# Per-bucket sums with the operands of TensorE exchanged, and a transpose in the last part

## The chip, the cores and the metric

The kernel runs on one core of a Trainium2 chip. The metric is the device time of one execution in microseconds; a kernel's time is the median of several timed runs. A further execution is profiled, and the views of the profile that are shown come from that one execution.

## The reference

The kernel computes one layer of a tensor-product message passing network on a graph with N = 10000 nodes and E = 640000 edges. Each node has a 64 x 4 matrix of features (C = 64 channels, M = 4 components), and all data is fp32.

```python
R = silu(edge_feat @ w_rad)                          # (E, C)
xs = x[src]                                          # (E, C, M)
tp = einsum('eci,ef,ifo->eco', xs, Y, cg)            # (E, C, M)
msg = R[:, :, None] * tp
agg = segment_sum(msg.reshape(-1, C * M), dst, N).reshape(N, C, M)
return einsum('ncm,cd->ndm', agg, w_mix)
```

The kernel doesn't form `tp` edge by edge. For each node n it first sums the outer product of R * x[src] (64 x 4 = 256 numbers) with Y (4 numbers) over the edges that end in n, and applies `cg` and `w_mix` afterwards, once for each node.

## The kernel before

The edges are first sorted by their destination. Two passes do this: `pass1` sorts the edges into groups of 576 nodes (18 buckets), `pass2` sorts each group into its 18 buckets of 32 nodes. Both use `route`: one-hot matrices (made at lines 546, 552 and 553) move the edges' payloads with matmuls on TensorE (line 560), and an indirect DMA from the GpSimd queue stores the moved rows (line 571). An edge's payload is nine words: a key, the four of Y and the four edge features.

The edges are taken in three parts (26%, 47% and 27% of them; `SPLIT`), so that the sorting of one part can run beside the sums of another. In `messages` the work is cut into units. A unit is one bucket's worth of 4 (first and second part) or 5 (last part) tiles of 128 edges; in the second part a bucket has two units. There are 313 buckets, so 313 + 626 + 313 = 1252 units with 5321 tiles in all. For a unit k the stages are:

- `gather`: one indirect DMA a tile from the GpSimd queue fetches x[src] into `xg` (line 785), six units ahead; there are eight buffers of `xg`.
- `turn`, `turned`, `radial`, `silu`: the payload is transposed on TensorE (line 798), copied on ScalarE (803), multiplied with `w_rad` on TensorE (808) and put through SiLU on ScalarE (811).
- `spots`: VectorE makes `S` = onehot(dst) * Y (lines 819 and 822), 32 nodes by 4 = 128 columns a tile.
- `products`: VectorE multiplies `xg` by R in place (line 829); the result is called `V`, 256 columns a tile.
- `sums`: TensorE adds up V^T S over the unit's tiles into `G` in PSUM (line 840). V is the stationary operand, in two halves of 128 columns (32 channels each), and S the moving one, so each tile takes two matmuls. `G` holds channel and component on the partitions and nodes by f on the columns.
- `fetch`, `evict`: `G` leaves PSUM. In the first part ScalarE copies it (line 871); in the second and last part VectorE adds the sum that was kept from the part before (line 869), which `fetch` has read from DRAM (854). After the first and second part the sum goes back to DRAM (873). In the last part it goes into `Gs`, which collects four buckets.
- `full`, `mix`, `mixed`: in the last part, once `Gs` has four buckets, TensorE multiplies it with the combined weights of `cg` and `w_mix` (line 888), ScalarE copies the result (896) and SP stores it.

The order of TensorE, VectorE and ScalarE is written out by hand in this stretch: the program emits the stages in four quarters for each k, each stage for its own unit k + a, and between two quarters `groups` inserts steps of the sorting. Within an engine the instructions run in that order. The quarters are, before the change:

```python
        quarters = (((index, LI), (gather, LG), (fetch, 4), (turn, 2), (sums, 0), (silu, 1)), ((turned, 2), (spots, 1)),
                    ((products, 1), (evict, 0)), ((radial, 2), (full, -1)))
```

`G` has one PSUM buffer, so the sum of the next bucket waits until the last one is evicted. Waits between engines are set by the framework, from the tiles that instructions read and write.

Of the kernel before, what the change touches and what calls it, by code (L numbers as in the profile page):

```python
# [18 lines left out]
F = mybir.dt.float32  # L19
# [3 lines left out]
AF = mybir.ActivationFunctionType  # L23
AX = mybir.AxisListType

P = 128
B = 18
# [4 lines left out]
NB = 32  # L32
# [3 lines left out]
SPLIT = ((0.26, (4,)), (0.47, (4, 4)), (0.27, (5,)))  # L36
LG = 6
LI = 8
# [33 lines left out]
class Kernel:  # L72
    def __init__(self, ctx, tc, x, src, dst, Y, ef, w_rad, cg, w_mix, out):
# [53 lines left out]
        self.p1.dst = self.dr.tile([self.p1.rows, self.p1.rw], F, name="grp")  # L127
        self.p2.dst = self.dr.tile([self.p2.rows, self.p2.rw], F, name="bkt")

        self.sums = self.dr.tile([self.NBK, P, 256], F, name="sums")  # L130
        self.in_group = {"grp": 0, "bkt": 0}
        self.tab = {}
        self.held, self.wanted, self.pos = None, False, None
# [607 lines left out]
    def messages(self):  # L741

        nc, ph = self.nc, self.ph
        units = [((k, g), j, s) for k, g in self.segs for j in range(self.nb(g)) for s in range(len(SPLIT[k][1]))]
        MT = max(sum(u) for _, u in SPLIT)
        n = len(units)
        IDX, XG, PRE, ST_, RT, SS, VS, GP, GS, OLD = ({} for _ in range(10))

        def quad(k):

# [4 lines left out]
        def tiles(k):  # L755

            g, j, s = units[k]
            u = SPLIT[g[0]][1]
            return sum(u[:s]), u[s]
# [71 lines left out]
        def sums(k):  # L831
            g, j, s = units[k]
            ut = tiles(k)[1]
            if s == 0:
                GP[g, j] = self.ps.tile([P, 2, NB, 4], F, name="G", tag="G", bufs=1)
            G = GP[g, j]
            V, S = VS.pop(k), SS.pop(k)
            for t in range(ut):
                for h in range(2):
                    nc.tensor.matmul(G[:, h].rearrange("p n f -> p (n f)"),  # L840
                                     V[:, t, 32 * h:32 * h + 32, :].rearrange("p c i -> p (c i)"),
                                     S[:, t].rearrange("p n f -> p (n f)"),
                                     start=(s + t + h == 0), stop=(last(k) and t == ut - 1),
                                     skip_group_check=True)

        def last(k):
            return units[k][2] == len(SPLIT[units[k][0][0]][1]) - 1

        def fetch(k):

            g, j, s = units[k]
            if g[0] and s == 0:
                OLD[g, j] = ph.tile([P, 2, 4, NB], F, name="old", bufs=4)
                nc.sync.dma_start(OLD[g, j].rearrange("p h f n -> p (h f n)"), self.sums[g[1] * B + j])

        def evict(k):
            g, j, s = units[k]
            if not last(k):
                return
            final = g[0] == len(SPLIT) - 1  # L860
            if not final:
                to = ph.tile([P, 2, 4, NB], F, name="Gp")
            else:
                if j % 4 == 0:
                    GS[g, j // 4] = ph.tile([P, 2, 4, 4, NB], F, name="Gs")
                to = GS[g, j // 4][:, :, :, j % 4, :]
            G = GP.pop((g, j)).rearrange("p h n f -> p h f n")
            if g[0]:
                nc.vector.tensor_tensor(to, OLD.pop((g, j)), G, op=OP.add)  # L869
            else:  # L870
                nc.scalar.activation(to, G, AF.Copy)
            if not final:
                nc.sync.dma_start(self.sums[g[1] * B + j], to.rearrange("p h f n -> p (h f n)"))

        def full(k):
            g, j, s = units[k]
# [15 lines left out]
        def mixed(k, po):  # L892
# [4 lines left out]
            nc.sync.dma_start(self.out[n0:n0 + nn, :], ot[:nn])  # L897


        quarters = (((index, LI), (gather, LG), (fetch, 4), (turn, 2), (sums, 0), (silu, 1)), ((turned, 2), (spots, 1)),  # L900
                    ((products, 1), (evict, 0)), ((radial, 2), (full, -1)))
        todo, po = [], None
        for k in range(-LI, n + 3):
            for stages in quarters:
# [218 lines left out]
```

## Time and profile before

| what | value |
|---|---|
| timed runs, median of 3 | 10905.27 us (10901.35 to 10920.43) |
| profiled execution, its own time | 10989.96 us |
| its span | 10987.9 us |
| granted TensorE clock, mean | 0.834 of full speed |
| busy: PE, PEld, DVE, ACT, POOL | 8420.1, 7126.3, 7056.8, 4102.8, 6003.7 us |
| matmul passes and weight loads | 52157 each |
| indirect gathers of x | 5321 |

PE is TensorE's matmuls and PEld its weight loads, which overlap them; DVE is VectorE, ACT is ScalarE, POOL is GpSimd, SP is the queue of the direct DMAs. Matmuls are pipelined, so that the busy time of PE is more than the time its columns take. In the groups of instructions a row gives line, engine, operation, what is written from what, shapes, how often, then busy time and the mean of one in ns, then the idle time of the engine just before and what ended it. "issue" is idle time in which the engine waited for nothing that the profile shows, "remote" a wait whose end is not put down to an instruction. An fp32 matmul shows as two passes, each with a weight load.

### The profile page before, as it was taken

Reading aid. Unit: us, or ns where it says so; the run is one execution under the profiler, and the core shown is the slowest. Engines: PE = TensorE matmul, PEld = TensorE weight load, DVE = VectorE, ACT = ScalarE, POOL = GpSimd, SP = SyncE. Lnnn points to the kernel's source line nnn. Section 1 sums busy time; section 2 is a strip of 40 time slices with the busy share of each in tenths; the row PEclk is TensorE's granted clock in tenths of the full one; section 3 lists DMA queues with packets and bytes.
Section 4 is the critical chain, followed back from the end, with each engine's and each line's share of the span. In section 5 each row is a group of like instructions: output and inputs, shape, how many; then the busy total and the mean of one; then the engine's idle time right before and its main releaser. Section 6 shows DMA issues by size and latency. Waiting matters only on the chain. (4 is left out here: it accounts for less than half of the span.)

```text
span 10987.9 us, 150963 instructions
## 1 busy us (share of the span) xinstructions
PE 8420.1 (77%) x52157; PEld 7126.3 (65%) x52157; DVE 7056.8 (64%) x13530; ACT 4102.8 (37%) x12301; POOL 6003.7 (55%) x6286
## 2 busy tenths in 40 slices
PE   6767787777877777777767777777767888888886
PEld 5656676666765666666656666666656666666665
DVE  7767777777766666666656666665546655656553
ACT  5645454554543433333333333333313222222220
POOL 1235455555555555555555556565566666666664
PEclk8878888888888888888888788888878888888887
DMA  7222222222223333333333333333333333333332
GB/s 155 77 62 80 83 84 86 83 82 85 87 84 93 96 99 98 99 98 99 99 94 97 92 95 102 98 103 97 96 110 103 106 107 107 104 104 107 107 103 86
DMA packets 695214, 1057.15 MB, mean 96 GB/s; under 512 B 251068, under 2 KB 499025, under 8 KB 694448
## 3 DMA queue, kind: packets, MB, share of 16 engines
q0 software_dynamic: 285872, 746.46, 23.6%
q1 hardware_dynamic: 405984, 294.29, 9.6%
q8 instruction: 413, 6.77, 0.3%
q10 hardware_dynamic: 2592, 6.74, 0.2%
q14 instruction: 353, 2.89, 0.1%
HBM read 856.14 MB, written 206.13 MB: 97 GB/s over the span
## 5 line engine op out<-in xcount | busy, mean ns | idle before, releaser
L785 POOL DMA_INDIRECT xg<-in_x_dram,sidx x5321 | 5052.2, 949 | 3344.1 <-issue 1371.8
L840 PE MATMUL G<-S,xg 128*128 128x128 f32 x21284 | 3250.8, 313 | 681.0 <-issue 395.4
L840 PEld LDWEIGHTS G<-S,xg 128*128 128x128 f32 x21284 | 3053.5, 226 | 797.3 <-issue 461.7
L560 PE MATMUL pr<-X,oh 128*128 128x126 f32 (+1 forms) x21252 | 3097.7, 306 | 604.6 <-ACT rt L567 294.1
L560 PEld LDWEIGHTS pr<-X,oh 128*128 128x128 f32 x21252 | 2929.4, 217 | 800.6 <-issue 384.2
L829 DVE TENSOR_TENSOR xg<-xg,pre 128x1024 f32<-128x1024 f32 (+1 forms) x1252 | 1603.8, 1281 | 866.8 <-ACT pre L811 705.8
L537 DVE TENSOR_TENSOR X<-dv,Wt 128x1485 f32<-128x1485 f32 (+3 forms) x941 | 1596.0, 1696 | 699.4 <-remote 413.2
L552 ACT ACTIVATE sq<-i,rowf 128x128 f32<-128x128 f32 x5640 | 1743.6, 393 | 5.6 <-DVE rowf L524 4.8
L811 ACT ACTIVATE pre<-pre 128x256 f32<-128x256 f32 (+1 forms) x1252 | 477.5, 381 | 2998.4 <-remote 990.0
L808 PE MATMUL pre<-wr,sT 36*128 36x256 f32 (+1 forms) x2504 | 1020.4, 490 | 310.1 <-ACT sT L803 256.4
L822 DVE TENSOR_TENSOR S<-dv,pay 128x512 f32<-128x512 f32 (+1 forms) x1252 | 907.6, 725 | 280.0 <-remote 131.0
L553 ACT ACTIVATE oh<-sq,ones 128x768 f32<-128x768 f32 (+1 forms) x941 | 928.5, 987 | 152.9 <-remote 50.9
L571 POOL DMA_INDIRECT grp<-rt,idx x417 | 415.2, 996 | 921.3 <-ACT rt L567 498.7
L571 POOL DMA_INDIRECT bkt<-rt,idx x524 | 524.8, 1002 | 646.6 <-ACT rt L567 422.0
L546 DVE TENSOR_TENSOR oh<-dv,rowf 128x768 f32<-128x768 f32 (+2 forms) x939 | 803.5, 856 | 0.3 <-PE pre L798 0.2
L808 PEld LDWEIGHTS pre<-wr,sT 36*128 36x128 f32 (+1 forms) x2504 | 414.6, 206 | 514.4 <-ACT sT L803 290.3
L567 ACT ACTIVATE rt<-pr 128x135 f32<-128x135 f32 (+1 forms) x941 | 253.6, 270 | 1075.9 <-remote 636.0
L869 DVE TENSOR_TENSOR Gs<-old,G 128x256 f32<-128x256 f32 x313 | 131.5, 420 | 766.5 <-PE G L840 277.9
L798 PE MATMUL pre<-ident,pay 128*36 128x128 f32 (+1 forms) x1252 | 383.2, 306 | 129.1 <-DVE xg L829 97.5
L798 PEld LDWEIGHTS pre<-ident,pay 128*36 128x36 f32 (+1 forms) x1252 | 132.7, 106 | 515.0 <-issue 235.5
L507 ACT ACTIVATE pc<-pp 128x432 f32<-128x432 f32 (+4 forms) x471 | 237.9, 505 | 559.7 <-remote 176.2
L803 ACT ACTIVATE sT<-pre 36x128 f32<-36x128 f32 (+1 forms) x1252 | 325.5, 260 | 285.6 <-PE pre L798 128.5
(214 smaller groups left out, 5164.6 us busy)
## 6 DMA issues: line engine op xcount, KB each, us to landing
xg<-in_x_dram,sidx POOLq DMA_INDIRECT x5321
sums<-Gp SPq DMA_DIRECT2D x626, 128.0 KB
old<-sums SPq DMA_DIRECT2D x626, 128.0 KB
bkt<-z SPq DMA_DIRECT2D x24, 994.5 KB
grp<-z SPq DMA_DIRECT2D x17, 679.5 KB
Wt<-grp SPq DMA_DIRECT2D x17, 679.5 KB
pay<-bkt SPq DMA_DIRECT2D x17, 648.0 KB
ys<-in_Y_dram SPq DMA_DIRECT2D x104, 96.0 KB
```

What stands on the lines that cost most here:

```text
L537: nc.vector.tensor_tensor(X[:, :m, :].rearrange("p t (s w) -> p t s w", w=W), msk.unsqueeze(3).to_broadcast([P, m, ps.r, W]), QD[c // Q][1 ...
L546: nc.vector.tensor_tensor(oh[:, :v, :], self.v128.unsqueeze(1).to_broadcast([P, v, P]), row[:, o:o + v].unsqueeze(2).to_broadcast([P, v, P ...
L552: nc.scalar.activation(sq[:, u, :], self.i128, AF.Square, bias=to, scale=-1.0)
L553: nc.scalar.activation(oh[:, v:v + len(at), :], sq[:, :len(at), :], AF.Relu, bias=self.ones[:, 0:1], scale=-2.0)
L560: nc.tensor.matmul(pr[:, :ps.rw], oh[:, u, :], X[:, u, :], start=(u == 0), stop=(not on and u == m - 1))
L571: st = nc.gpsimd.indirect_dma_start(out=ps.dst, out_offset=bass.IndirectOffsetOnAxis(ap=idx[:, i:i + 1], axis=0), in_=RT.pop(c), in_offset ...
L785: nc.gpsimd.indirect_dma_start(out=xg[:, t, :], out_offset=None, in_=self.x, in_offset=bass.IndirectOffsetOnAxis(ap=si[:, u:u + 1], axis=0))
L798: nc.tensor.transpose(pre[:ut * W, 384:512], pb, self.ident)
L808: nc.tensor.matmul(R, ST_.pop(k)[:ut * W], self.wr[:ut * W, :ut * 64], start=True, stop=True)
L822: nc.vector.tensor_tensor(S[:, :ut], self.eq[:, :ut].unsqueeze(3).to_broadcast([P, ut, NB, 4]), pb[:, :, 1:5].unsqueeze(2).to_broadcast([P ...
L829: nc.vector.tensor_tensor(V, V, R.unsqueeze(3).to_broadcast([P, ut, 64, 4]), op=OP.mult)
L840: nc.tensor.matmul(G[:, h].rearrange("p n f -> p (n f)"), V[:, t, 32 * h:32 * h + 32, :].rearrange("p c i -> p (c i)"), S[:, t].rearrange( ...
```

## The change

The sums exchange their operands: S[:, t] (128 columns) becomes the stationary operand and V[:, t] with its 256 columns the moving one. Each tile takes one matmul instead of two, and `G` now holds nodes by f on the partitions and channel and component on the columns. In the first two parts nothing else follows than that the kept sums have this layout in DRAM; the evictions are plain copies or additions. In the last part, where `mix` needs channel and component on the partitions, the evicted sum (`Gp` in SBUF) is transposed: `flip` does two transposes on TensorE for the unit before, right after the sums, and `flipped` copies the result on ScalarE into `Gs`, in the third quarter. For this `G` becomes one tile of a whole PSUM bank with two halves of 256 columns that are handed out in turn, to sums and to transposes alike.

```diff
--- before.py
+++ after.py
@@ -127,7 +127,7 @@
         self.p1.dst = self.dr.tile([self.p1.rows, self.p1.rw], F, name="grp")
         self.p2.dst = self.dr.tile([self.p2.rows, self.p2.rw], F, name="bkt")
 
-        self.sums = self.dr.tile([self.NBK, P, 256], F, name="sums")
+        self.sums = self.dr.tile([self.NBK, NB * 4, 256], F, name="sums")
         self.in_group = {"grp": 0, "bkt": 0}
         self.tab = {}
         self.held, self.wanted, self.pos = None, False, None
@@ -744,7 +744,12 @@
         units = [((k, g), j, s) for k, g in self.segs for j in range(self.nb(g)) for s in range(len(SPLIT[k][1]))]
         MT = max(sum(u) for _, u in SPLIT)
         n = len(units)
-        IDX, XG, PRE, ST_, RT, SS, VS, GP, GS, OLD = ({} for _ in range(10))
+        IDX, XG, PRE, ST_, RT, SS, VS, GP, GS, OLD, GE, GT = ({} for _ in range(12))
+
+
+        bank = self.ps.tile([P, 2, 256], F, name="G", tag="G", bufs=1)
+        turns = itertools.cycle((0, 1))
+        half = lambda: bank[:, next(turns), :]
 
         def quad(k):
 
@@ -832,16 +837,12 @@
             g, j, s = units[k]
             ut = tiles(k)[1]
             if s == 0:
-                GP[g, j] = self.ps.tile([P, 2, NB, 4], F, name="G", tag="G", bufs=1)
+                GP[g, j] = half()
             G = GP[g, j]
             V, S = VS.pop(k), SS.pop(k)
             for t in range(ut):
-                for h in range(2):
-                    nc.tensor.matmul(G[:, h].rearrange("p n f -> p (n f)"),
-                                     V[:, t, 32 * h:32 * h + 32, :].rearrange("p c i -> p (c i)"),
-                                     S[:, t].rearrange("p n f -> p (n f)"),
-                                     start=(s + t + h == 0), stop=(last(k) and t == ut - 1),
-                                     skip_group_check=True)
+                nc.tensor.matmul(G, S[:, t].rearrange("p n f -> p (n f)"), V[:, t].rearrange("p c i -> p (c i)"),
+                                 start=(s + t == 0), stop=(last(k) and t == ut - 1), skip_group_check=True)
 
         def last(k):
             return units[k][2] == len(SPLIT[units[k][0][0]][1]) - 1
@@ -850,27 +851,41 @@
 
             g, j, s = units[k]
             if g[0] and s == 0:
-                OLD[g, j] = ph.tile([P, 2, 4, NB], F, name="old", bufs=4)
-                nc.sync.dma_start(OLD[g, j].rearrange("p h f n -> p (h f n)"), self.sums[g[1] * B + j])
+                OLD[g, j] = ph.tile([P, 256], F, name="old", bufs=4)
+                nc.sync.dma_start(OLD[g, j], self.sums[g[1] * B + j])
 
         def evict(k):
             g, j, s = units[k]
             if not last(k):
                 return
-            final = g[0] == len(SPLIT) - 1
-            if not final:
-                to = ph.tile([P, 2, 4, NB], F, name="Gp")
-            else:
-                if j % 4 == 0:
-                    GS[g, j // 4] = ph.tile([P, 2, 4, 4, NB], F, name="Gs")
-                to = GS[g, j // 4][:, :, :, j % 4, :]
-            G = GP.pop((g, j)).rearrange("p h n f -> p h f n")
+            to = ph.tile([P, 256], F, name="Gp")
+            G = GP.pop((g, j))
             if g[0]:
                 nc.vector.tensor_tensor(to, OLD.pop((g, j)), G, op=OP.add)
             else:
                 nc.scalar.activation(to, G, AF.Copy)
-            if not final:
-                nc.sync.dma_start(self.sums[g[1] * B + j], to.rearrange("p h f n -> p (h f n)"))
+            if g[0] < len(SPLIT) - 1:
+                nc.sync.dma_start(self.sums[g[1] * B + j], to)
+            else:
+                GE[k] = to
+
+        def flip(k):
+
+            if k not in GE:
+                return
+            Ge = GE.pop(k)
+            GT[k] = half()
+            for h in range(2):
+                nc.tensor.transpose(GT[k][:, h * P:(h + 1) * P], Ge[:, h * P:(h + 1) * P], self.ident)
+
+        def flipped(k):
+            g, j, s = units[k]
+            if k not in GT:
+                return
+            if j % 4 == 0:
+                GS[g, j // 4] = ph.tile([P, 2, 4, 4, NB], F, name="Gs")
+            nc.scalar.activation(GS[g, j // 4][:, :, :, j % 4, :],
+                                 GT.pop(k).rearrange("p (h n f) -> p h f n", h=2, f=4), AF.Copy)
 
         def full(k):
             g, j, s = units[k]
@@ -897,8 +912,8 @@
             nc.sync.dma_start(self.out[n0:n0 + nn, :], ot[:nn])
 
 
-        quarters = (((index, LI), (gather, LG), (fetch, 4), (turn, 2), (sums, 0), (silu, 1)), ((turned, 2), (spots, 1)),
-                    ((products, 1), (evict, 0)), ((radial, 2), (full, -1)))
+        quarters = (((index, LI), (gather, LG), (fetch, 4), (turn, 2), (sums, 0), (flip, -1), (silu, 1)),
+                    ((turned, 2), (spots, 1)), ((products, 1), (evict, 0), (flipped, -1)), ((radial, 2), (full, -1)))
         todo, po = [], None
         for k in range(-LI, n + 3):
             for stages in quarters:
```

## The prediction

> **What bounds the kernel now.** I read the page first: span, busy shares, the chain that ended last, the costliest groups.
>
> ```profile
> span 10987.9 us, 150963 instructions
> PE 8420.1 (77%) x52157; PEld 7126.3 (65%) x52157; DVE 7056.8 (64%) x13530; ACT 4102.8 (37%) x12301; POOL 6003.7 (55%) x6286
> issue 0%; DMA 0%; POOL 0%; DVE 0%; POOLq 0%; SPq 0%
> L785 POOL DMA_INDIRECT xg<-in_x_dram,sidx x5321 | 5052.2, 949 | 3344.1 <-issue 1371.8
> L840 PE MATMUL G<-S,xg 128*128 128x128 f32 x21284 | 3250.8, 313 | 681.0 <-issue 395.4
> L840 PEld LDWEIGHTS G<-S,xg 128*128 128x128 f32 x21284 | 3053.5, 226 | 797.3 <-issue 461.7
> ```
>
> No engine is full, and the chain is lost within the last microseconds, so the bound has to be read from the waits. The sums at line 840 are the largest group of TensorE. Each fp32 matmul is two passes: 5321 tiles by two halves by two is 21284.
>
> ```profile
> POOL xg L785 <- issue: 1371.8, 4404, 7.2
> POOL xg L785 <- PE G L840: 1068.8, 325, 12.1
> PEld G L840 <- DVE Gp L869: 155.4, 96, 8.0
> PEld G L840 <- DVE Gs L869: 95.2, 52, 8.1
> PEld G L840 <- ACT Gp L871: 61.5, 25, 6.6
> DVE Gp L869 <- remote: 224.6, 53, 8.3
> DVE Gs L869 <- remote: 218.8, 56, 8.6
> ```
>
> The first two rows say who leads. A gather costs its queue 0.949 us and an issue gap of 1371.8 / 4404 = 0.31 us, 1.26 us in all, and still the queue stands 1068.8 us waiting for the sums to release a buffer. So the loop through TensorE, VectorE and ScalarE is behind the gathers for a good part of the time, and what shortens or lengthens it moves the end. The windows say how much room there is in the last part, where the change adds work:
>
> ```profile
> core 0: us, PE busy (x) PEld busy (x) DVE busy (x) ACT busy (x) POOL busy (x), PEclk, DMA share, GB/s
> 8400.00:10960.00 2560.00, 2062.98 (x11887) 1695.03 (x11885) 1475.73 (x2702) 645.49 (x1922) 1553.40 (x1632) 0.84 0.36 105
> ```
>
> The 1632 transfers of POOL need 1632 x 1.26 = 2056 us of these 2560, so 504 us could be won before the gathers bind, and ScalarE is three quarters idle. Now the timeline, for the pitch of the passes and for their irregularities:
>
> ```profile
> 9612.02 2.40 PE L840 MATMUL G<-S,xg 128*128 128x128 f32 x20
> 9617.31 0.42 DVE L869 TENSOR_TENSOR Gs<-old,G 128x256 f32<-128x256 f32 x1 [3.38 <-remote]
> 9621.07 3.72 PE L888 MATMUL po<-wf,Gs 128*128 128x256 f32 x16
> 9629.08 0.36 PE L840 MATMUL G<-S,xg 128*128 128x128 f32 x1 [0.48 <-issue]
> 9630.47 0.27 PE L840 MATMUL G<-S,xg 128*128 128x128 f32 x1 [1.03 <-issue]
> 9631.89 0.37 PE L840 MATMUL G<-S,xg 128*128 128x128 f32 x1 [1.16 <-issue]
> ```
>
> Twenty passes of 128 columns take 2.40 us: less one tail of about 0.3, that is 0.11 us a pass, with a weight load under each. Sixteen passes of 256 columns (line 888) take 3.72 us, 0.22 us a pass. The pitch goes by columns and the load is hidden. But there are also places where the sums drip out one pass in 1.4 us with nothing to wait for ("issue"), and the eviction at 9617.31 starts 2.9 us after the sums' last pass (9612.02 + 2.40) although it waits for nothing else that is shown. These two are what the number of instructions could touch.
>
> **The change, part by part.**
>
> *Matmul form.* 21284 passes of 128 columns become 10642 of 256, and as many weight loads go. Columns stay: 16 x 0.11 = 1.76 us for four tiles before, 8 x 0.22 = 1.76 us after. I price this at 0; what hides the loads that go is the passes themselves. A page speaks the other way: the Trainium skill, "TensorE: Matmul & The Clock Gate", section "Back-to-back issue gap", gives about 81 ns a matmul sustained at 128 columns and 131 ns at 512, because the loads count at small widths; by it, wide passes would be cheaper per column, up to half of the group and more. This trace disagrees (0.11 against 0.22), and the trace decides.
>
> *Issue gaps.* Of the 395.4 us, by part:
>
> ```profile
> PE G L840 <- issue: 395.4, 448, 6.6
> PE G L840 <- issue: 159.3, 159, 6.6
> PE G L840 <- issue: 173.0, 221, 1.9
> L888 PE MATMUL po<-wf,Gs 128*128 128x256 f32 x1104 | 275.4, 406 | 0.0
> L888 PE MATMUL po<-wf,Gs 128*64 128x256 f32 x272 | 77.8, 450 | 25.8 <-issue 23.5 <-ACT colsbkt L338 1.6 <-DVE Gs L869 0.6
> ```
>
> (whole run, the stretch 3700 to 8300, the stretch 8400 to 10700). That is 18.6 ns a pass. The 256-column passes of line 888, in the same stretch, have 0.0 in 1104 and 25.8 us in 272, 18.8 ns a pass over both: so between half (10642 x 18.8 = 200 us left) and all of it goes, 195 to 395 us. I take 300, nearer to the full-width row, whose shape the new one has. What follows when the gaps go is the gathers, with their room of 504 us in the last part, so most of it passes to the end; I count 0.8: **-240** (ends -156 and -316; 0 if the gaps don't belong to the form).
>
> *Late completions.* TensorE's 104314 instructions (52157 twice) lose 42568 / 2 = 21284 and gain 1252: 19% fewer. The evictions' waits on "remote" are 224.6 + 218.8 = 443 us; were they to go with the number of instructions, 19% is 84 us, half of that on the path: **-45** (ends 0 and -84).
>
> *Evictions.* They no longer reorder. The reordering copy took 374 ns, the plain one of the same size 383:
>
> ```profile
> L871 ACT ACTIVATE Gp<-G 128x256 f32<-128x256 f32 x313 | 117.0, 374 | 312.3 <-PE G L840 164.7 <-remote 77.3 <-PE pre L798 24.2
> L896 ACT ACTIVATE ot<-po x87: 362/383/384, 8411.3 to 10939.0; 128x256 f32<-128x256 f32 x69, 64x256 f32<-64x256 f32 x17, 80x256 f32<-80x256 f32 x1
> L869 DVE TENSOR_TENSOR Gs<-old,G 128x256 f32<-128x256 f32 x313 | 131.5, 420 | 766.5 <-PE G L840 277.9 <-remote 218.8 <-PE pre L798 199.2
> L798 PE MATMUL pre<-ident,pay 128*36 128x128 f32 (+1 forms) x1252 | 383.2, 306 | 129.1 <-DVE xg L829 97.5
> 10000.11 0.27 PE L798 MATMUL pre<-ident,pay 128*45 128x128 f32 x1
> 10000.22 2.40 PE L840 MATMUL G<-S,xg 128*128 128x128 f32 x20
> ```
>
> So 0. The transfers of `sums` and `old` on SP keep their number and size, and nothing on SP or POOL is moved past anything: 0.
>
> *Transposes, last part only.* 313 units by two, 626 on TensorE. The nearest row, the transposes of line 798, has 306 ns busy and a pitch of 0.11 us to the next group. Between these I take 0.15, near the pitch, since two follow each other: 94 us. TensorE is busy 81% of that stretch and half of the rest is not its own choice, so half counts: **+47** (ends 0 and 626 x 0.306 = +192).
>
> *The second copy.* 313 copies on ScalarE at 0.383 us are 120 us, hidden by ScalarE's idle 1915 us in the last part: **0**, and +120 if that cover is gone. Behind a copy that waits for the transposes stand, on ScalarE, the sort's one-hot squares and the next unit's SiLU, which has a whole unit (2560 / 313 = 8.2 us) until its products are due.
>
> *New waits.* Sums and transposes share one bank. In the last part the two half-turns make every sum land in the same half again, and the next sum waits for the eviction (now behind the transposes, 0.3 us) and for the copy (0.38): 0 to 0.68 us a unit, 0 to 213 us. TensorE's sort and radial matmuls usually lie between; the row "PEld G <- DVE Gs" has 52 waits in 313 units, one in six, so 213 / 6: **+36**. Behind that wait on TensorE stand the sort's moves and the next radial matmul. The mix (87 of them) read an eviction a unit old; now it reads a copy issued one quarter earlier, so TensorE can stand there: between 0 and 87 x 3.38 (the one late eviction above) = 294 us; I take 0.5 us each, nearer to a copy than to a late eviction: **+44**.
>
> Sum: -240 - 45 + 47 + 36 + 44 = -158 us. Against the profiled execution, 10989.96 us (its span and 2.1 us around), 10832. The median of the timed runs, 10905.27, lies 84.7 us below the profiled one: 10747 us.
>
> **The rivals.**
>
> *The gaps stay, the last part pays.* The gaps would then be TensorE waiting for something that has no link with its own passes; they'd reappear before the sort's matmuls or as late completions. For it: the evictions' "remote" waits exist where no pass drips, and the timed runs are only 84.7 us shorter than the profiled one, so I can't tell which gaps the profiling itself makes. Against it: line 888's 0.0. Then the price is 47 + 36 + 44 = +127, 11032 us. It decides from where less than 160 us of gap goes. This is the slower side.
>
> *The halves do overlap.* If the sum of the next bucket may start in the other half while the first is read, the waits on Gp (155.4 + 61.5 = 217 us) in the first two parts go as well: 0.8 x 217 = 174 more, 10573 us. For it: the code alternates the halves. Against it: it is one tile, and every user waits by tile as far as this trace shows. The Trainium skill, "PSUM — Partial Sum Buffer", section "PSUM bank collisions raise a hardware error", says that two engines must be kept apart by bank, not by address; by that rule the waits stay, and no run here shows it yet.
>
> *It cancels.* Gaps halve (-156) and the waits in the last part come out at twice my price: within 22 us of 10905. That the change doesn't do what it says, a form that still issues two passes per 128 columns, would end here too or above; the two rows of line 888 speak against it.
>
> **How the numbers follow.** Forecast 0.50, halves overlap 0.08, cancels 0.08, gaps stay 0.34. Faster by over 0.2% (22 us, about what can be told from no change) is 0.58, the same 0.08, slower 0.34. The forecast alone, with its ends, goes from 10905 - 316 - 84 + 0 = 10505 to about 10880. The range reaches down to that, which takes in 10573, and up over 11032 to 11060, leaving out the dearest mixes.
>
> **What would show it.** In the profile after: 10642 passes of 256 columns at a 0.22 us pitch, issue gaps before the sums under 200 us, POOL's waits on the sums under 900 us; 626 transposes with ScalarE copies behind them, and TensorE's waits on these copies under 100 us in the last part. Wrong, if the gaps stay near 395 us or move to line 560, if the last part (8400 to 10960) grows by over 150 us, or if TensorE's waits on Gp vanish.

## The result and the profile after

| kernel | median | range | runs |
|---|---|---|---|
| before | 10919.39 us | 10889.62 to 10941.35 | 14 |
| changed | 10957.44 us | 10926.13 to 10977.64 | 14 |

The changed kernel takes 1.004 of the time of before (95% interval 1.003 to 1.005), 38 us more. The profiled execution of it took 10961.29 us. That of before, 10989.96 us, lies above all 14 of before's timed runs, so differences of some tens of us between the two profiles are not evidence. Shifts of hundreds of us in a row are, where a second profile of both kernels (before_again and after_again, below) repeats them.

The page of the changed kernel, its span, engines and the groups that answer to those of before:

```profile
span 10959.2 us, 130913 instructions
PE 8206.1 (75%) x42141; PEld 6426.0 (59%) x42141; DVE 7053.4 (64%) x13530; ACT 4199.3 (38%) x12614; POOL 6024.7 (55%) x6286
L790 POOL DMA_INDIRECT xg<-in_x_dram,sidx x5321 | 5071.0, 953 | 3220.5 <-issue 1372.3
L844 PE MATMUL G<-xg,S 128*128 128x256 f32 x10642 | 2971.9, 430 | 234.6 <-issue 104.3
L844 PEld LDWEIGHTS G<-xg,S 128*128 128x128 f32 x10642 | 2211.1, 218 | 599.4 <-issue 111.4
```

On TensorE the forecast of the passes and of the gaps came true: 10642 passes, and the issue gaps before the sums fell from 395.4 us to 104.3. The timeline of the last part shows the new order (start, duration, row):

```profile
9604.78 2.32 PE L844 MATMUL G<-xg,S 128*128 128x256 f32 x10
9606.94 0.38 PE L879 MATMUL G<-ident,Gp 128*128 128x128 f32 x2
9607.25 0.80 PE L813 MATMUL pre<-wr,sT 45*128 45x320 f32 x2
```

Ten passes from 9604.78 to the start of the transposes at 9606.94 are 2.16 us, 0.22 us a pass, as forecast; the pair of transposes holds TensorE for 0.31 us. Where, then, is the gain? In the waits. These rows of before were not shown yet (engine, line, whom it waited for, total us, times, longest):

```profile
ACT pre L811 <- remote: 990.0, 163, 13.5
DVE xg L829 <- ACT pre L811: 705.8, 248, 12.0
ACT rt L567 <- remote: 636.0, 90, 14.0
DVE X L537 <- remote: 413.2, 81, 14.9
PE pr L560 <- ACT rt L567: 294.1, 121, 11.0
```

The same rows after, and with them the waits that the prediction priced:

```profile
DVE xg L834 <- ACT pre L816: 1007.7, 298, 12.6
POOL xg L790 <- PE G L844: 979.5, 318, 12.1
ACT pre L816 <- remote: 861.3, 113, 12.6
ACT rt L567 <- remote: 860.1, 109, 16.9
DVE X L537 <- remote: 558.3, 86, 18.4
PE pr L560 <- ACT rt L567: 520.0, 130, 10.6
DVE Gp L864 <- remote: 392.0, 87, 10.5
ACT Gs L887 <- DVE Gp L864: 489.5, 185, 11.8
PEld po L903 <- ACT Gs L887: 75.6, 44, 9.8
PEld G L844 <- DVE Gp L864: 69.9, 68, 9.3
PEld G L844 <- ACT Gs L887: 43.4, 43, 3.6
PEld G L844 <- ACT Gp L866: 28.8, 14, 6.5
```

TensorE lost 291 us of gaps before the sums and gained 226 us of waiting at line 560, for ScalarE's copy `rt` of the sort. ScalarE in turn gained 224 us at this copy on "remote", and VectorE 145 us at `X`, one step of the same sort. The second profiles repeat these three shifts: 294.6 and 504.8 us, 586.1 and 904.7, 389.5 and 639.5. Other remote waits fell, SiLU's from 990.0 us to 861.3 and the evictions' from 443 to 392.0; all the remote rows among the view's 199 largest add up to 3,828 us before and 3,898 after (3,949 and 4,224 in the second profiles). What line 567 waits for is TensorE's own move of the payloads: the result stands, its completion comes late. So the delay has not gone with the passes. Much of it sits at another place of the loop.

The last part did not grow by the 150 us that would have spoken against the forecast: `Gs` is written from 8370.5 to 10934.8 us before and from 8357.4 to 10907.4 us after, 2,564 and 2,550 us. The window of 2560 us that the prediction showed now has less of TensorE (2062.98 us before) and more of ScalarE (645.49):

```profile
8400.00:10960.00 2560.00, 2017.96 (x9341) 1539.16 (x9339) 1467.51 (x2716) 738.99 (x2223) 1549.42 (x1623) 0.87 0.36 104
```

### The profile page after: what moved, and what is told of

It is laid out like the page before. It is cut to its first block, busy times and chain, and to the rows that moved or that the text cites. A ratio compares the mean times of both kernels' runs of the same rounds, so it can differ in the third digit from the quotient of the medians.

```text
span 10959.2 us, 130913 instructions
## 1 busy us (share of the span) xinstructions
PE 8206.1 (75%) x42141; PEld 6426.0 (59%) x42141; DVE 7053.4 (64%) x13530; ACT 4199.3 (38%) x12614; POOL 6024.7 (55%) x6286
## 5 line engine op out<-in xcount | busy, mean ns | idle before, releaser
L844 PE MATMUL G<-xg,S 128*128 128x256 f32 x10642 | 2971.9, 430 | 234.6 <-issue 104.3
L844 PEld LDWEIGHTS G<-xg,S 128*128 128x128 f32 x10642 | 2211.1, 218 | 599.4 <-issue 111.4
L816 ACT ACTIVATE pre<-pre 128x256 f32<-128x256 f32 (+1 forms) x1252 | 478.4, 382 | 2278.7 <-remote 861.3
L864 DVE TENSOR_TENSOR Gp<-old,G 128x256 f32<-128x256 f32 x626 | 261.9, 418 | 867.6 <-remote 392.0
L567 ACT ACTIVATE rt<-pr 128x135 f32<-128x135 f32 (+1 forms) x941 | 254.7, 271 | 1235.4 <-remote 860.1
L903 PE MATMUL po<-wf,Gs 128*128 128x256 f32 (+2 forms) x1392 | 367.8, 424 | 83.7 <-ACT Gs L887 47.6
```

The lines of the kernel that those rows point to most:

```text
L844: nc.tensor.matmul(G, S[:, t].rearrange("p n f -> p (n f)"), V[:, t].rearrange("p c i -> p (c i)"), start=(s + t == 0), stop=(last(k) and ...
```

## The theories

- **A**, the forecast's: the gaps belong to the form, what TensorE saves passes to the end, and the last part's new steps give it back.
- **B**, the first rival: gaps and late completions are one disturbance, independent of the sums' own passes. It takes back what they save, and the last part's chain is all that is left to measure.
- **C**, formed on the way: the exchanged form makes it worse. In the compiled program a run of sums posts its completion (the semaphore update that other engines wait for) once for a unit if the last matmul of the run has no wait of its own. In the old form that is so (second half of the last tile): the trace of before has 1,252 posts of the sums. In the exchanged form each of the 5,321 matmuls waits for its own gather, and nearly all post for themselves, 5,281 in the trace of the changed kernel and 5,321 in that of form_only.

In the expectations of after_again, fewer_gathers and old_on_pe, which are older, C stands for another guess: that the gathers' queue sets the time where before takes 8900 us.

## The experiments

The runs were made in groups, each on one chip, and a whole group shows one of two conditions: before takes about 8,900 us in it, or 10,890 to 10,980 us, as in the runs of the prediction. The expectations speak of a chip of 8900 or of 10900 us; but two chip numbers stand with both, so it is not shown to be a property of the chip, and I call it the condition. A ratio always compares with before of the same group.

| run | before there | ratio (95% interval) |
|---|---|---|
| form_only | 8900.61 | 0.9983 (0.9975 to 0.9992) |
| last_part_only | 8900.61 | 0.9999 (0.999 to 1.0008) |
| half_sums | 8900.61 | 0.9934 (0.9921 to 0.9947) |
| copy_on_dve | 8900.61 | 0.999 (0.9981 to 0.9999) |
| before_again | 10983.72 | 0.9999 (0.9985 to 1.0012) |
| after_again | 10983.72 | 1.0054 (1.0035 to 1.0073) |
| fewer_gathers | 10983.72 | 0.8799 (0.878 to 0.8818) |
| old_on_pe | 10983.72 | 1.0029 (1.0016 to 1.0042) |
| form_only_2 | 10892.39 | 1.0018 (1.0004 to 1.0032) |
| last_part_only_2 | 10892.39 | 1.0028 (1.0012 to 1.0043) |
| before_split_v | 10892.39 | 1.0639 (1.0615 to 1.0662) |
| form_split_v | 10892.39 | 1.0393 (1.037 to 1.0416) |
| form_few_posts | 8898.1 | 1.0002 (0.9993 to 1.0011) |
| form_only_3 | 8898.1 | 0.9985 (0.9976 to 0.9994) |
| after_few_posts | 8898.1 | 1.0003 (0.9994 to 1.0012) |
| form_few_posts_2 | 10973.39 | 1.0002 (0.9991 to 1.0012) |
| half_sums_2 | 8895.29 | 0.9938 (0.9924 to 0.9951) |
| half_sums_3 | 8902.37 | 0.9938 (0.9925 to 0.9952) |

**The form alone and the last part alone.** `form_only` is the changed kernel without `flip` and `flipped`, so that `Gs` holds the sums in the exchanged layout; its second run is the same kernel in the 10,900 condition, its third in the 8,900 one.

```diff
             G = GP.pop((g, j))
+            if g[0] == len(SPLIT) - 1:
+                nc.vector.tensor_tensor(GS[g, j // 4][:, :, :, j % 4, :],
+                                        OLD.pop((g, j)).rearrange("p (h f n) -> p h f n", h=2, f=4),
+                                        G.rearrange("p (h n f) -> p h f n", h=2, f=4), op=OP.add)
+                return
...
-                    ((turned, 2), (spots, 1)), ((products, 1), (evict, 0), (flipped, -1)), ...
+                    ((turned, 2), (spots, 1)), ((products, 1), (evict, 0)), ...
```

`last_part_only` keeps halves, transposes and copies, and undoes the exchange, so that the transposes turn sums that were already the right way round.

```diff
-                nc.tensor.matmul(G, S[:, t]..., V[:, t]..., ...)
+                for h in range(2):
+                    nc.tensor.matmul(G[:, h * P:(h + 1) * P], V[:, t, 32 * h:32 * h + 32, :]..., S[:, t]..., ...)
```

> Leaves out: the transposes and the second copy of the last part (its sums enter the mix untransposed); the exchanged matmul form and the bank with two halves stay. Theory A (the forecast's: the gaps before the sums' passes go and four fifths of that reaches the end; the last part's additions eat it): about 0.97 of before, 10600 to 10700 us. Theory B (the passes drip because TensorE's completions are held back, and the hold doesn't shorten; what the sums save, the next matmuls, copies and SiLUs wait): 0.99 to 1.00 of before, with the issue gaps before the sums gone and the waits on ScalarE's copies before the sort's matmuls longer.

> The changed kernel with the matmul form of the sums undone (V stationary, two matmuls of 128 columns a tile), so that the transposes, second copies and new waits of the last part stand alone; the sums are transposed once too often, the amount of work is what counts. Theory A: 1.012 of before (+127 us), or as much as 1.03 if the form really gained 285 us and the changed kernel still ends 38 us above. Theory B: 1.003 to 1.010, that is what the changed kernel shows or a little more, with ScalarE's wait for the evictions before the second copy (489.5 us in the changed kernel) again in the last part.

In the 8,900 condition the page of last_part_only, in the old form with all its 21,284 passes, reads:

```profile
span 8899.9 us, 152197 instructions
L845 PE MATMUL G<-S,xg 128*128 128x128 f32 x21284 | 2875.2, 294 | 245.9 <-DVE Gp L867 167.3
```

The idle time before the sums is led by the eviction, not by issue. The waits view of this run, and of form_only, has no row that ends in remote. Gaps and late completions come together and go together, with the condition and not with the form. That is the first hard evidence against A's main term. (Both expectations for last_part_only, 1.003 and more, were written for a kernel with late completions and missed.) Now one kernel in both conditions, form_only and then form_only_2 (the page's rows for sums, sort, SiLU and gathers):

```profile
span 8884.5 us, 129583 instructions
L790 POOL DMA_INDIRECT xg<-in_x_dram,sidx x5321 | 5058.1, 951 | 1855.4 <-issue 1327.1
L844 PE MATMUL G<-xg,S 128*128 128x256 f32 x10642 | 2821.2, 414 | 311.9 <-DVE Gp L871 169.2
L560 PE MATMUL pr<-X,oh 128*128 128x126 f32 (+1 forms) x21252 | 2749.2, 287 | 135.6 <-DVE oh L546 79.6
L816 ACT ACTIVATE pre<-pre 128x256 f32<-128x256 f32 (+1 forms) x1252 | 477.1, 381 | 1894.0 <-PE pre L813 1638.7
```

```profile
span 10911.8 us, 129583 instructions
L790 POOL DMA_INDIRECT xg<-in_x_dram,sidx x5321 | 5062.3, 951 | 3122.5 <-issue 1405.1
L844 PE MATMUL G<-xg,S 128*128 128x256 f32 x10642 | 3015.8, 435 | 300.9 <-issue 119.3
L560 PE MATMUL pr<-X,oh 128*128 128x126 f32 (+1 forms) x21252 | 3104.4, 306 | 874.1 <-ACT rt L567 470.8
L816 ACT ACTIVATE pre<-pre 128x256 f32<-128x256 f32 (+1 forms) x1252 | 477.1, 381 | 2831.0 <-remote 918.8
```

The same 129,583 instructions: gathers and SiLU last as long in both (951 and 381 ns), while TensorE idles 739 us more before line 560 and SiLU's 918.8 us are on remote. That completions come late shows in the instructions' own times too: of the 1,252 SiLUs, 225 in form_only_2 start more than 1 us after both their matmul and ScalarE's activation before them have ended, by 1,036 us together, and one in form_only. The other way round, from ScalarE's copy `sT` to TensorE's radial matmul, no start in either run is late by more than 0.3 us. In the 8,900 condition the gathers' queue idles only 1855.4 us before gathers, of which 1327.1 are its own issue: it is nearly full, and the sums are worth little.

> The changed kernel without its extra steps in the last part: the sums take onehot(dst) * Y as stationary and 256 columns of R * x[src], the last eviction writes straight into Gs on VectorE, nothing is transposed. It ran on a chip where the kernel before takes 8900 us, at 0.998; what it does where the kernel before takes about 10950 us is open. Theory A (the forecast's: the idle time before the sums is worth most of its 300 us there, and the last part gives it back): 0.975 to 0.985. Theory B (late completions set the time, and the idle time only moves in front of other matmuls): 0.998 to 1.004. Theory C (the exchanged form makes each of 5,321 matmuls post its own completion where 1,252 posted before, and that lengthens the lateness): 1.003 to 1.010. Where the chip is one of 8900 us, all three say 0.997 to 1.000.

> The changed kernel with its sums back in the form of before (halves of one bank, transposes, eviction and copy in the last part stay): 1,252 of the sums' matmuls post. At 1.000 on a chip of 8900 us. Where the kernel before takes 10950 us: theory A says 1.015 to 1.025 (the last part gives back what the form gains), theory B 1.002 to 1.006 (the last part's chain of sums, eviction, transpose and copy is all of the change's 0.4 to 0.5 per cent), theory C 0.998 to 1.002 (the posts of the form are what costs).

With 1.0018 and 1.0028, the parts add up to 1.0046, between the two measurements of the whole (1.004 and 1.0054). Each is in B's interval; A's 0.975 to 0.985 is far off. The form alone gives nothing although its gaps fell to 119.3 us. In last_part_only_2, gaps and late completions stand side by side:

```profile
ACT rt L567 <- remote: 763.7, 107, 16.9
ACT Gs L890 <- DVE Gp L867: 713.9, 229, 10.3
PE G L845 <- issue: 299.6, 366, 5.3
```

The gaps of the old form are back (299.6), and remote at the sort's copy is less (763.7) than in form_only_2 (956.3, which led line 567 there) and more than before's 636.0.

> The exchanged form alone once more, 5,321 posts, to be held against form_few_posts on one chip: 1.000 to 1.004 on a chip of about 10900 us, 0.997 to 1.000 on one of 8900 us, by every theory.

It repeats form_only within its interval.

**Half of the sums, and the copy moved.** `half_sums` is before with the sums over every other tile (the rest is left out); `copy_on_dve` is the changed kernel with the second copy on VectorE.

```diff
-            for t in range(ut):
+            for t in range(0, ut, 2):
```

> The kernel before, with the sums taken over every second tile only: 10016 of 21284 passes stay out, about 1100 us of passes at 0.11 us and half of the issue gaps. It tells what TensorE's time in the sums is worth at the end. Theory A (0.8 of what the sums save reaches the end): 0.90 of before, about 9900 us. Theory B: a third of it or less, 0.97 or above.

```diff
-            nc.scalar.activation(GS[g, j // 4][:, :, :, j % 4, :], GT.pop(k)..., AF.Copy)
+            nc.vector.tensor_copy(GS[g, j // 4][:, :, :, j % 4, :], GT.pop(k)...)
```

> The changed kernel with the second copy (transposed sum into the mix's operand) on VectorE, right behind the eviction, instead of on ScalarE. Theory A (the last part's cost is the matmuls' and copies' own time): 1.004 of before or a little above, like the changed kernel, since 313 copies move to a busier engine. Theory B (the cost is ScalarE standing behind the eviction, with the SiLUs and one-hot squares behind it): under the changed kernel by 20 us or more, 0.998 to 1.002 of before.

Where completions come in time, about half of the sums is worth 0.7 per cent. That kernel also shows that a low granted clock alone does not bring the late completions: its mean was 0.818, lower than before's 0.834 of the first profile, at a span of 8838.0 us and without a remote row. The same program, though, had a mean of 0.900 as form_only and 0.832 as form_only_2, so what part the clock has in the difference of the two conditions stays open. copy_on_dve, the whole change but for the place of one copy, stands between form_only and last_part_only there. The expectations of both runs were written for the 10,900 condition, so between A and B neither decides anything.

half_sums ran twice more, in the 8,900 condition again, with 0.9938 both times; in the 10,900 condition neither it nor copy_on_dve has run.

> The kernel before with the sums over every other tile only (half of their matmuls, more exactly the even tiles of each unit, left out otherwise), all else as it was. The sums take some 3,000 us of TensorE and 395 us of gaps on a chip of 10900 us, so some 1,400 us of TensorE's time go. The forecast's price (0.8 of what TensorE saves reaches the end): 0.87 to 0.92. Lateness takes back what TensorE saves (theory B): 0.985 to 1.000. Something between, 0.94 to 0.975, would say that TensorE's busy time counts and only the gaps do not. On a chip of 8900 us: 0.992 to 0.995, as half_sums gave there.

> The kernel before with the sums over every other tile only, once more. On a chip of about 10900 us: the forecast's price (0.8 of what TensorE saves reaches the end) says 0.87 to 0.92; theory B (lateness takes back what TensorE saves) 0.985 to 1.000; between them, 0.94 to 0.975, busy time counts and gaps do not. On a chip of 8900 us: 0.992 to 0.995.

**What the lateness goes with.** `before_again` and `after_again` are the two kernels unchanged. `fewer_gathers` is before with the first gather of each unit, 1,252 of 5,321, replaced by a direct transfer of fixed rows (so that these products are of wrong rows).

```diff
+                if t == 0:
+                    nc.sync.dma_start(xg[:, t, :], self.x[:P])
+                    continue
                 nc.gpsimd.indirect_dma_start(
```

> The kernel before, unchanged, for its profile on the chip of these runs: the last four runs had it at 8900.61 us where it took 10919.39 before, and showed neither issue gaps before the sums nor late completions. If the gaps and the late completions belong to the chip and not to the kernel, this trace, where the time is near 8900, has issue gaps before the sums under 50 us and evictions that start within 0.1 us of the sums' end when VectorE is free; where it is near 10900, it has both.

> The changed kernel, unchanged, beside the kernel before on the chip of these runs. Theory B (a late completion holds the next engine whatever the passes do): near 10900 it repeats 1.003 to 1.005. Where the kernel before is near 8900 there is no hold, and the gathers' queue is 94% filled by 1.21 to 1.26 us each, so theory C (gathers bind there): 0.998 to 1.001. Theory A would give under 0.98 near 10900 and has nothing to win near 8900.

> The kernel before with one gather in each unit (1252 of 5321) replaced by a direct transfer of 128 fixed rows of x on SP: same bytes to the same tile, wrong rows; the GpSimd queue is relieved of 1252 x 1.26 = 1577 us. Theory C (near 8900 the gathers' queue binds): 0.87 to 0.93 of before there. If TensorE, VectorE and ScalarE's loop bound instead: 0.97 or above. Near 10900, where POOL stands waiting for the sums for 1000 us, theory B says 0.95 to 1.0.

The waits of before_again, then of fewer_gathers:

```profile
ACT pre L811 <- remote: 1094.2, 175, 13.0
ACT rt L567 <- remote: 586.1, 87, 14.1
PE G L840 <- issue: 388.9, 446, 6.8
```

```profile
ACT pre L814 <- remote: 468.0, 116, 10.2
ACT rt L567 <- remote: 227.2, 51, 11.5
PE G L843 <- issue: 94.5, 146, 3.7
```

The number of the sums' passes is the same. Yet with 24 per cent fewer gathers the issue gaps before them fell by three quarters and both remote waits by more than half, and the time by 12 per cent. So here these gaps go with the gathers and not with the passes. B had said 0.95 to 1.0 for this condition, and missed: 1252 x 1.26 us, by the first rows of the prediction, are some 1,578 us less for the gathers' own queue, and 1,318 us of time went. What in the gathers matters, this one run can't tell, since the rows were fixed and another queue moved them. And they can't be the whole cause: in the 8,900 condition all 5,321 gathers run without a late completion.

**The new form in two parts only.** `old_on_pe` sums the last part in the old form, and TensorE adds the kept sum by an identity matmul, so that neither transposes nor second copies are needed.

```diff
+            if g[0] == len(SPLIT) - 1:
+                old = OLD.pop((g, j))
+                for h in range(2):
+                    nc.tensor.matmul(G[:, h * P:(h + 1) * P], old[:, h * P:(h + 1) * P], self.ident, ...)
+                for t in range(ut):
+                    ...
```

> A version that keeps the exchanged form in the first two parts and needs no transposes of the new sum: in the last part the sums have the form of before, and the kept sum is added by TensorE itself (a matmul of it against the identity, two a bucket), so the eviction is one reordering copy on ScalarE and VectorE's 313 additions go. 626 fp32 matmuls come, 1252 passes, 138 us at 0.11 us. Theory B and C: 0.996 to 1.000 of before, and 0.003 to 0.006 under the changed kernel near 10900, since ScalarE no longer stands behind the eviction and TensorE no longer behind the second copy. Theory A: 0.98.

1.0029: without any chain of transpose and copy it is still not faster than before. That is above the 0.996 to 1.000 of B, and 0.0025 under the changed kernel of the same group, where 0.003 to 0.006 were expected. ScalarE's copy `rt` waits 925.4 us on remote in this run, the largest of its remote waits.

**The posts.** Two pairs test C. In `before_split_v` and `form_split_v` the products go to a tile of their own; a matmul then has no gather to wait for, and both forms post about as often (1,201 and 1,135). The room for it is taken from `xg`.

```diff
-LG = 6
+LG = 5
...
-            V = VS[k] = XG.pop(k)[:, :ut]...
+            X = XG.pop(k)[:, :ut]...
+            V = VS[k] = ph.tile([P, UT, 64, 4], F, name="V", bufs=2)[:, :ut]
```

> The kernel before with the products written to a tile of their own (two buffers) instead of over xg, with 6 buffers of xg and gathers 5 units ahead (8 and 6 before; the room is what it frees). A gather then waits for VectorE's products and no longer for the sums on TensorE, and the sums post 1,201 completions (1,252 before). If the gathers' wait for late completions of the sums (some 1,030 us in the kernel before) is what carries the lateness to the end: 0.95 to 0.985 on a chip of 10950 us. If the lateness reaches the end by the chain of radial part, silu, products and sort all the same: 0.995 to 1.01. On a chip of 8900 us: 0.99 to 1.005, the queue of gathers being full there.

> The exchanged form without the last part's extra steps (as form_only_2), and with the products in a tile of their own as in before_split_v; here the sums post 1,135 completions although each is one matmul. To be held against before_split_v of the same chip: theory C says that it is faster than that by over 0.5 per cent where completions are late, as the extra completions are gone and the shorter instruction list stays; theory B says that they agree within 0.4 per cent; theory A says that it is faster by 1.5 to 2.5 per cent, and form_only_2 as well.

No expectation had 1.0639. The waits of before_split_v and then of form_split_v say what it cost and what the form did there:

```profile
ACT pre L811 <- remote: 1524.4, 214, 16.4
POOL xg L785 <- DVE V L830: 1227.1, 313, 13.7
PE G L841 <- issue: 483.6, 420, 11.2
```

```profile
POOL xg L790 <- DVE V L835: 1084.4, 315, 13.5
ACT pre L816 <- remote: 978.0, 136, 15.9
PE G L845 <- issue: 329.3, 192, 8.0
```

The gathers now wait 1,227 us for the products, which wait for SiLU, which waits longer on remote: the late completion is passed on in another way. But in this arrangement the form is worth 2.3 per cent: 11331.88 / 11596.19 = 0.977, by the ends of the two intervals 0.973 to 0.981. That agreed with A's figure for this pair and, the posts being nearly equal, with C; B, which allowed 0.4 per cent, missed here. A's other half, that form_only_2 gains as much, had not come. So I put C to the test in the kernel's own arrangement. `form_few_posts` is form_only with the last tile of a unit in two matmuls of 128 columns, of which the second waits for nothing: 1,252 posts again, as in the old form, with 6,573 matmuls.

```diff
-            for t in range(ut):
+            for t in range(ut - 1):
                 nc.tensor.matmul(G, S[:, t]..., V[:, t]..., ...)
+            for h in range(2):
+                nc.tensor.matmul(G[:, h * P:(h + 1) * P], S[:, ut - 1]..., V[:, ut - 1, 32 * h:32 * h + 32, :]..., ...)
```

`after_few_posts` does the same to the changed kernel.

> The exchanged form alone (as form_only_2), but the last tile of each unit is added as two matmuls of 128 columns: the second of them waits for nothing, so one post stands for the unit, 1,252 in all instead of 5,321; 6,573 matmuls instead of 5,321 (10,642 before), no other difference. Theory C (the posts of single matmuls keep completions late and eat the gain): 0.975 to 0.992 on a chip of about 10900 us, 1 per cent or more below form_only_3. Theory B (lateness follows the gathers and takes back whatever TensorE gains): within 0.3 per cent of form_only_3, 1.000 to 1.004. On a chip of 8900 us both say 0.997 to 1.000.

> The changed kernel whole, with the last tile of each unit added as two matmuls of 128 columns, so that the sums post 1,252 times as before. Theory C: 0.978 to 0.996 on a chip of about 10900 us, the last part's 0.3 per cent above form_few_posts. Theory B: 1.003 to 1.007, as the changed kernel itself. On a chip of 8900 us: 0.997 to 1.001.

> The kernel of form_few_posts again (exchanged form alone, the last tile of a unit in two matmuls, 1,252 posts of the sums). On a chip where the kernel before takes about 10900 us: theory C 0.975 to 0.992, theory B 1.000 to 1.004, as form_only_2 gave 1.0018 there. On a chip of 8900 us again 0.999 to 1.001.

The first two ran in the 8,900 condition, where form_few_posts is 0.17 per cent above form_only_3 and so does not gain by its fewer posts. In the other, where before takes 10,973 us, it gave 1.0002 (0.9991 to 1.0012). C's 0.975 to 0.992 falls. This run and form_only_2 (1.0018) lie 0.0016 apart, in two groups and with intervals that overlap; that the posts cost more than this is not shown. The waits of that run:

```profile
ACT pre L816 <- remote: 1160.3, 161, 12.0
ACT rt L567 <- remote: 895.5, 117, 15.6
PE G L847 <- issue: 75.3, 102, 1.8
PE G L844 <- issue: 74.1, 68, 4.8
```

With 149 us of gaps instead of some 390, few posts, and no transposes, the time is that of before; the remote wait at `rt` is 895.5 us instead of 586 to 636. Of the three, B is what stands in this arrangement, with its misses in fewer_gathers and form_split_v.

## Why the prediction was wrong

It said 10747 us and faster; it came out 38 us slower. The measured median lies inside the range, near its upper end, above the 10880 that the forecast alone reached; only the dearer rival held the range open so far. By its own steps:

- **Matmul form, 0.** Right: 0.22 us a pass for 256 columns. The Trainium skill, "TensorE: Matmul & The Clock Gate", section "Back-to-back issue gap", would have made the wide passes cheaper per column; without late completions the sums' busy time fell from 2875.2 us in the old form to 2821.2 us, 2 per cent, so the measurement decides against it here.
- **Issue gaps, -240.** The step that failed. Its first half was right, and even its size: 291 us went, 300 were taken. The second, that 0.8 of it "passes to the end" because the gathers have room, was wrong: the form alone is 1.0018, +20 us (0.0018 x 10892; +4 to +35 by the interval). In its place TensorE waited 226 us longer at line 560 for the sort's copy, which itself waited 224 us longer for completions of TensorE. What I read as a cost of passes was one face of a disturbance that is absent in the other condition with the same passes, and that fell by three quarters with fewer gathers and unchanged passes. My end "0 if the gaps don't belong to the form" was the case. (The gathers' price was also a little high: 4404 of the 5321 had the issue gap, so the mean is 1.21 us and not 1.26, and the room in the last part about 590 us and not 504. With more room the step would have looked safer still.)
- **Late completions, -45.** Wrong too. I let them go with the number of instructions. The evictions' remote waits, from which I took the term, did fall, from 443 to 392.0 us. But with 19 per cent fewer passes ScalarE's at `rt` rose from 636.0 to 860.1 us, and all remote rows together went from 3,828 to 3,898 us, so nothing was saved.
- **Evictions, 0.** Nothing speaks against it: 418 ns after, 420 before.
- **Transposes, +47; copy, 0; new waits, +36 and +44.** Together +127; last_part_only_2 measured 0.0028 x 10892 = +30 us (+13 to +47), and nothing in the 8,900 condition. As times on their engines the terms were of the right order: 0.31 us a pair of transposes (0.30 taken), 43.4 us of the sums' loads waiting on the copy (36), 75.6 us of the mix's loads (44). As shares of the end they were too dear, by the same error as the gain: time on TensorE is not time of the kernel. The one wait I did not price is the copy's on the eviction, 489.5 us on ScalarE; most of it was hidden, for last_part_only_2 has 713.9 us of it and lost some 30 us in all.

  The copy reads the other half of the bank and needs nothing of that eviction; the program holds a wait for it all the same. The Trainium skill, "PSUM — Partial Sum Buffer", section "PSUM bank collisions raise a hardware error", asks for a guard by bank and quadrant, by bank in the simple version, and not by address; the wait agrees with the rule, though no run here shows what would happen without it.
- **The rivals.** "The gaps stay, the last part pays" came nearest, not by gaps that stayed before the sums, but in its words "they'd reappear before the sort's matmuls or as late completions", with the price of the last part too high. I had its best evidence in hand: evictions waiting on remote where no pass drips. Against it I had set line 888's 0.0, a row that only said that wide passes drip less, not that the time is saved. "The halves do overlap": the loads' waits on Gp fell from 217 to 99 us but did not vanish, and the time did not follow them either.
- **What would show it.** Gaps under 200 held. The loads' waits on the copies came to 119.0 us (43.4 + 75.6), over the 100, and POOL's waits on the sums to 979.5, over the 900. At line 560, where I had said that gaps would prove me wrong, the idle time rose by waits on `rt`; the issue gaps there stayed, 236.3 us before and 253.5 after.

**What stays open.** Why completions come late in some groups of runs, with the same program, and not in others, no run shows. Nor why the form is worth 2.3 per cent where the gathers wait for VectorE's products, and nothing where they wait for the sums. Whether much more time taken off the sums would reach the end in the 10,900 condition is not known; half_sums has only run in the other. No version beats before in both conditions: form_only is 0.15 to 0.17 per cent faster in one and 0.18 slower in the other. And the two traces of form_only's program differ in their records of semaphore updates, 157,386 in form_only and 59,978 in form_only_2; whether updates were merged or not recorded can't be seen, so the label "remote" may in part hang on the recording, though the late starts of SiLU do not.

## What to carry to other kernels

An idle time marked "issue" before a long run of matmuls is a price of that run only if it goes with the run: look first whether other places of the same trace show waits that nothing explains ("remote"), and if they do, take both for one disturbance and price its removal at zero until a run says otherwise. A saving on an engine that nobody finds full should be carried step by step to the wait that it shortens, and a share such as 0.8 needs a row of its own. And measure the parts of a change in the same condition as the whole: here the same program took 8,900 or 10,900 us, and terms that count in one condition are nothing in the other.

## What the runs showed of the hardware

- One program, 8884.5 us in one group of runs and 10911.8 us in another. The mean time of a SiLU on ScalarE and of a gather on GpSimd does not differ (381 and 951 ns in both); TensorE's completions are seen late (remote waits of 918.8 us before SiLU against none) and its passes drip (119.3 us of issue gaps before the sums against none in the view). The granted clock was 0.900 in the one and 0.832 in the other; but half_sums, with 0.818 at 8838.0 us, has no late completions, so a low clock alone doesn't bring them.
- In one run the lateness went with the indirect gathers: 24 per cent fewer of them, and remote before SiLU fell from 1094.2 to 468.0 us. It needs more than them: with all 5,321 and 8884.5 us there is none.
- Two engines do not read the two halves of one PSUM bank side by side in this program, as it holds a wait between them: 489.5 us of ScalarE standing behind VectorE's eviction of the other half, 713.9 us with the old form.
